# A pre-norm attention and GEGLU block: VectorE's additions of a split exp given to accumulating DMAs, more tiles for VectorE, and a second chunk cut in two

## The chip, the cores and the metric

The kernel runs on one core of a Trainium2 chip. A core has a matrix engine (TensorE, PE in the profile), VectorE (DVE), ScalarE (ACT), GpSimd (POOL) and SyncE (SP, which here only starts DMAs), each with its own queue of instructions that it works through in order; semaphores order the engines among each other. The metric is the device time of one execution in microseconds, the median of several runs.

## The reference

For 2048 rows of 640 numbers in bf16 (batch 1, 32 heads of 20):

```
x  = A_x
n  = layernorm(x)                       # no gain, no bias
q, k, v = split(n @ wqkv)               # 32 heads of 20
p  = softmax(q k^T / sqrt(20))          # 2048 x 2048 per head
h  = x + concat(p v) @ wo
m  = layernorm(h)
h2 = h + (gelu_tanh(m @ w_gate) * (m @ w_up)) @ w_down   # inner width 1728
```

The scores are 32 x 2048 x 2048 = 134 million numbers, and each goes through an exp.

## The kernel before

**Units of work.** Queries are worked on in chunks (`SIZES`: 512, 512, 256, 256, 256, 128, 128 rows). Four heads make a group, whose four small products lie side by side in TensorE. A tile is one PSUM bank of scores of one head: 128 keys on the partitions, 512 columns, which are 512 queries of one key block, or 256 queries of two key blocks, or 128 of four. A quad is the tiles of one group and key block for its four heads. A slot is one group of a chunk of 512, two groups of a chunk of 256, four of a chunk of 128: always 16 quads or 64 tiles, and there are 32 slots, 2048 tiles. No maximum is taken from the scores: a bound per query is put into one row of the operands beforehand.

**Two engines make the exp.** Most tiles go to ScalarE, two or three banks in one instruction (`unit`, the `exp` activation). Slots in `SIX` (8 to 15) use six banks for scores, in two halves of three; where a tile for VectorE is due there, it takes the third bank of the unit, and ScalarE's instruction takes two. In the other slots the halves have three and two banks, and VectorE's tile goes to bank 7 or 5, which the background work shares. `D_QUADS` says how many quads of each slot go to VectorE (68 in all, 272 tiles), `D_LEAD` how many tiles ahead of their slot these begin: 24 for most slots from slot 11 on.

**VectorE's exp** (`d_exp`) works in integer arithmetic on the bits of the number. L881 takes a tile out of PSUM, scaled, as int16 `v`. When two tiles (slots below `D_WIDE` = 18, "narrow", 128x1024) or four (from slot 18 on, "wide", 128x2048) are there, six instructions follow: `df` is the fraction of `v`'s bits; `dw` a linear function of it; `dw` squared; `dw` times `df`; `v` plus `dw`; and a scaling of `v` by 0.25 with an offset (called the rescaling below), after which the bits are those of a bf16 number. All six are on VectorE. The results are kept in a few buffers (`dv0`, `dv`, `dvw`) until the product with V takes them, at least `D_LAG` units later.

**The background.** While exps run, TensorE also does the products of probabilities and V (`pv_op`, accumulated in bank 6), and behind each chunk `post`: the output projection, the layer norm (its root in a run of small instructions on POOL, `ln_rsqrt`), transposes by DMA on SP's queue, and the MLP: gate products, a copy by VectorE, one gelu for the chunk on ScalarE (which has to load another function table for it, and the exp's again behind it), up products, VectorE's multiplication, `down`, the store. At the end of the last chunk the same is done without other work beside it (`tail`).

**The order.** The program records all operations with their reads, writes, banks, priorities and assumed durations, and `Sched.schedule` plays them through once, taking on each engine the ready operation of the best priority. What comes out is a fixed order for each queue, with semaphore waits (`emit`). So a changed number in the tables at the top moves instructions on all engines. Where TensorE would be idle for long, the planner puts in fillers: products with zeros (`sc.pad`) or thrown away ones (`sc.warm`).

The lines that matter in the profile: L366 is the helper through which most instructions of VectorE, ScalarE and POOL are recorded; L947 the score products; L881 the evacuation of VectorE's tiles; L1039 the transposes of the attention output; L1048 its division; L663 the projections; L1120 the gate and up products; L1155 and L1169 their copies and multiplications by VectorE; L1200 and L1204 the down products and the last addition.

Of the kernel before, what the change touches and what calls it, by code (L numbers as in the profile page):

```python
# [307 lines left out]
D = 640  # L308
# [6 lines left out]
NG = H // 4  # L315
SIZES = (512, 512, 256, 256, 256, 128, 128)
BASE = (0, 0, 0, 2, 0, 2, 3)
SIX = tuple(range(8, 16))
CHUNKS = tuple((sum(SIZES[:i]), n) for i, n in enumerate(SIZES))
# [10 lines left out]
PV_QUADS = 2  # L330
D_LAG = 9
MERGE = ()
PR, PR2 = 12, 6
D_QUADS = (1,) + (2,) * 15 + (2, 2) + (3, 2) * 5 + (2, 2, 2, 2)
D_FIRST, D_PART = 2, 0.75
D_LEAD = ((0,) * 8, (0, 10, 20) + (24,) * 21)
D_WIDE = 18
# [7 lines left out]
def bass_sequential_preLN__mha_block__glu_gated_geglu__prompt_kernel(  # L345
# [12 lines left out]
    with ExitStack() as es:  # L358
# [3 lines left out]
        def sb(name, shape, dt=BF16):  # L362
            return es.enter_context(nc.sbuf_tensor(name, shape, dt))
# [16 lines left out]
        identf = sb("identf", [128, 128], FP32)  # L380
        sel = sb("sel", [128, NA, H])
        zer = sb("zer", [128, 32])
        sel0 = sb("sel0", [128, 4, 32])
        off0 = sb("off0", [128, 1], FP32)
# [15 lines left out]
        pts = sb("pts", [128, PR * 512])  # L400
        osb = sb("osb", [128, 2, 512], FP32)
        rc = sb("rc", [128, 2, 16], FP32)
        o_nat = sb("o_nat", [128, 4, D])
        sq = sb("sq", [128, 512])
        xn_t = sb("xn_t", [128, 2, D])
        dvx = sb("dvx", [128, 1024])

# [21 lines left out]
        qoff = carve(512)  # L429
        aq = [carve(512) for _ in range(2)] + [sq[:], xn_t[:, 0, 0:512], xn_t[:, 1, 0:512]]  # L430
        carve = carver(regw, W_WORDS)
# [24 lines left out]
        df1 = carve(1024)  # L456
        dw1 = carve(1024).bitcast(F16)
        carve = carver(qt_all[:, 0, :, :].rearrange("p g s -> p (g s)"), NG * 512)
        dvw += [carve(2048).bitcast(I16) for _ in range(2)]
        dv.append(dvx[:].bitcast(I16))  # L460
        zb = dvx[:].rearrange("p (i s) -> p i s", i=2)
        dv0 = [ha_f[:, 1024 * i:1024 * i + 1024].bitcast(I16) for i in range(5)]
        df0, dw0 = ha_f[:, 5120:6144], ha_f[:, 6144:7168].bitcast(F16)
        carve = carver(qt_all[:, 1, :, :].rearrange("p g s -> p (g s)"), NG * 512)
        df2 = carve(2048)
        dw2 = carve(2048).bitcast(F16)
        carve = carver(qt_all[:, 2, :, :].rearrange("p g s -> p (g s)"), NG * 512)
# [9 lines left out]
        def bank(b, n=512):  # L477
            return PS[:, 512 * b.b:512 * b.b + n]
# [7 lines left out]
        def cst(fn, key, n=128):  # L486
            op(POOL, fn, 0.1 + n * 0.001, P_BG, writes=[key, "pool"])
# [19 lines left out]
        for g in range(1, NG, 2):  # L507
            cst(I("memset", f32(qt_all[:, 0, g:min(g + 2, NG), :]), 0.0), "qf0%d" % g, 512)
        cst(I("memset", sel[:], -1.0), "sel", 160)
        cst(I("affine_select", out=sel[:], in_=sel[:], compare_op=ALU.is_ge, fill=0.0, base=0,  # L510
              pattern=[[128, NA], [-DH, H]], channel_multiplier=1), "sel", 160)
        cst(I("affine_select", out=sel[:], in_=sel[:], compare_op=ALU.is_ge, fill=0.0, base=DH - 1,
              pattern=[[-128, NA], [DH, H]], channel_multiplier=-1), "sel", 160)
        cst(I("memset", sel0[:], 0.0), "sel0")
        cst(I("memset", off0[:], 0.0), "off0", 1)
# [76 lines left out]
        def ln_apply(eng, src, dst, dkey, t, rkeys, prio, first=False):  # L592
            if eng == "act":
                fn = I("activation", dst, src, ACT.Identity, bias=nm[:, t:t + 1], scale=rs[:, t:t + 1])
            else:
                fn = I("tensor_scalar", dst, src, mu[:, t:t + 1], rs[:, t:t + 1], ALU.add if first else ALU.subtract,
                       ALU.mult)
            return op(eng, fn, 0.82 if eng == "act" else c_dve(D, 0.46), prio,
                      reads=list(rkeys) + [("mu", t), ("rs", t)] + ([("nm", t)] if eng == "act" else []), writes=[dkey])

# [67 lines left out]
        def aqk(t):  # L668
            return ("xn", t - 3) if t >= 3 else ("aq", t)

# [98 lines left out]
        def q_bound0(banks, prio):  # L769
            bk = Bank(*banks)  # L770
            key = ("bk", sc_id())
            w_readers.append(op("pe", lambda eng: eng.matmul(
                bank(bk), sel0[:].rearrange("p j e -> p (j e)"), aq[0], start=True, stop=True),
                c_mm(512), prio, mode="full", util=0.213, reads=[("aq", 0), "sel0"], writes=[key], acq=[bk]))
            dst = qt_all[:, 0, 0, :]
            q_first.append(op("dve", lambda eng: eng.scalar_tensor_tensor(
                out=dst, in0=bank(bk), scalar=off0[:, 0:1], in1=dst, op0=ALU.add, op1=ALU.add), c_dve(512) + 0.05, prio,
                reads=[key, "off0"] + q_keys[0][0], writes=[("qo", 0, 0)], rel=[bk]))
            q_keys[0][0] = [("qo", 0, 0)]
# [70 lines left out]
        d_last = {}  # L850
        d_cur = [None]
        d_late = []
        d_pv = {}
# [8 lines left out]
        def d_exp(b, tile, prio, u):  # L862
# [5 lines left out]
            if h == 0:  # L868
                busy = set(x[1][1] for x in d_done)
                pool = [(kind, i) for i in range(5 if kind != "w" or CHUNKS[slots[units[u][0][0]][0]][0] >= 1536 else 3)]  # L870
                pool = [p for p in pool if p not in busy]
                assert pool
                d_cur[0] = min(pool, key=lambda p: d_last.get(p, -1))
                d_last[d_cur[0]] = len(d_ops)
            i = d_cur[0]
            v = {"e": dv0, "l": dv, "w": dvw}[kind][i[1]]
            df, dw = {"e": (df0, dw0), "l": (df1, dw1), "w": (df2, dw2)}[kind]
            keys = [("dv", i)] + ([("dv", ("l", k)) for k in ((0, 1), (2, 3), ())[i[1]]] if kind == "w" and i[1] < 3 else [])
            aft = tuple(e_ops) + (q_done(0) if c else ()) + (q_done(1) + tuple(d_late) if kind == "w" else ()) + \
                (q_done(2) if kind == "w" and i[1] > 2 else ())  # L880
            d_ops.append(op("dve", lambda eng: eng.tensor_scalar(v[:, 512 * h:512 * h + 512], bank(b), EXP_MUL, -32000.0,  # L881
# [5 lines left out]
            if h < n - 1:  # L887
                return
            zi = df.bitcast(I16)
            w_ = len(d_raw) / 2  # L890
            d = lambda fn, n, r, w: d_ops.append(op("dve", fn, 0.066 + n * w_, prio, reads=r, writes=w))
            d(I("tensor_scalar", zi, v, 511, 2048, ALU.bitwise_and, ALU.bitwise_or), 0.265, [("dv", i)], ["df"])
            d(I("tensor_scalar", dw, zi, CA / OCT, CB, ALU.mult, ALU.add), 0.265, ["df"], ["dw"])
            d(I("tensor_tensor", dw, dw, dw, ALU.mult), 0.53, ["dw"], ["dw"])
            d(I("tensor_tensor", dw, dw, zi, ALU.mult), 0.53, ["df", "dw"], ["dw"])
            d(I("tensor_tensor", v, v, dw, ALU.add), 0.53, ["dw", ("dv", i)], [("dv", i)])
            d(I("tensor_scalar", v, v, 0.25, 16256.0 + 128.0 * (CC - 1.0), ALU.mult, ALU.add), 0.265, [("dv", i)], [("dv", i)])
# [126 lines left out]
        def epilogue(s_, bk, d_sums):  # L1024
# [3 lines left out]
            nt = nq // 128  # L1028
            op("dve", I("tensor_copy", osb[:, s, :], PS[:, 512 * 6:512 * 7]), c_dve(512), P_QK,
               reads=[("O", s_)], writes=[("osb", s)], rel=[bk], after=tuple(d_sums))  # L1030
            b2 = Bank(*BGC[c])
# [6 lines left out]
            for tt in range(4):  # L1038
                op("pe", lambda eng, tt=tt: eng.transpose(bank(b2)[:, tt * 128:(tt + 1) * 128],  # L1039
                                                          osb[:, s, tt * 128:(tt + 1) * 128], identf[:]),  # L1040
                   c_mm(128, 2.5), P_EPI, mode="full", reads=[("osb", s), "identf"], writes=[key], acq=[b2] if tt == 0 else [],
                   after=tuple(aft) if tt == 0 else ())
# [22 lines left out]
        def post(c, first_banks, banks, tail):  # L1065
# [33 lines left out]
            for tt in range(tb, tb + nt):  # L1099
                t = q0 // 128 + tt - tb  # L1100
                ln_apply("dve", h_sb[:, tt, :], xn_t[:, t % 2, :], ("xn", t % 2), t, [("h", tt, 0), ("h", tt, 1)], pd)
                if tail:
                    transposes(xn_t[:, t % 2, :], [("xn", t % 2)], hnT[:, :, tt * 128:(tt + 1) * 128], ("hnT", tt),
                               first_banks, p, "act", after=first)
                else:
                    dma_transposes(xn_t[:, t % 2, :], [("xn", t % 2)], hnT[:, :, tt * 128:(tt + 1) * 128], ("hnT", tt),
                                   after=first)
# [188 lines left out]
```

## Time and profile before

| | us |
|---|---|
| median of 3 runs (914.05 to 917.4) | 914.34 |
| profiled execution, own time | 916.19 |
| profiled execution, span | 914.2 |
| ScalarE busy | 881.1 (96%) |
| TensorE busy | 824.1 (90%) |
| VectorE busy | 794.1 (87%) |
| GpSimd busy | 48.2 (5%) |

The span is the time from the first to the last instruction of the profiled execution; its own time has what lies around the span as well. The first exp starts at 33.3 us, the last one ends at 881.6 us. Instructions of one engine overlap a little at their ends, so a mean duration is longer than the distance from one start to the next; a "pace" below is that distance. The granted TensorE clock was 0.998 of full speed.

In a line of a group, the columns are: source line, engine, operation, output and input tensor with shape and type, count, busy time, mean duration in ns, and the idle time of the engine just before these instructions with what ended it. In a timeline: start, duration, engine, line, operation. In a line of DMA issues: count, size of one, median us from issue to landing.

### The profile page before, as it was taken

To read this page: it belongs to the slowest core of one execution; us is meant where nothing else is said; L and a number is where in the kernel's file an instruction comes from. 1 tells how busy PE (TensorE), PEld (TensorE's weight loads), DVE (VectorE), ACT (ScalarE), POOL (GpSimd) and SP (SyncE) were. 2 spreads that over 40 slices of the span, in tenths; PEclk is the share of its full clock that TensorE was granted. 3 is DMA by queue.
4 is the path that set the end of the run, shared out by engine and by line. 5 is a ranking of instruction groups with operands and counts; after the bars stand their busy time and mean duration, and the time that the engine had idled before them with its cause. 6 is when DMAs were issued, how large, how long until landed. Compare 5 with 4: busy or idle time off the path is not lost.

```text
span 914.2 us, 22759 instructions
## 1 busy us (share of the span) xinstructions
PE 824.1 (90%) x9952; PEld 351.2 (38%) x10017; DVE 794.1 (87%) x1458; ACT 881.1 (96%) x789; POOL 48.2 (5%) x149
## 2 busy tenths in 40 slices
PE   3999999999898878899798989999999989998998
PEld 1432322222232222233233333344454445556666
DVE  8869998999899986987899997999998998779753
ACT  7999999999999999999999999999999999999982
POOL 5000000000011000000021000002010000010000
PEclk9999999999999999999999999999999999999999
DMA  7211020323801000000122000000100000110000
GB/s 259 83 31 33 23 62 25 90 67 76 291 25 30 1 1 1 1 8 16 37 35 27 1 1 1 16 30 10 37 16 18 29 1 3 36 27 10 10 17 15
DMA packets 39514, 34.33 MB, mean 38 GB/s; under 512 B 19436, under 2 KB 36936, under 8 KB 39416
## 3 DMA queue, kind: packets, MB, share of 16 engines
q1 hardware_dynamic: 39416, 32.89, 12.9%
q8 instruction: 78, 1.28, 0.6%
q14 instruction: 20, 0.16, 0.1%
HBM read 20.12 MB, written 8.09 MB: 31 GB/s over the span
## 4 chain that ended last, share of the span: by engine, by line
ACT 57%; PE 23%; DVE 17%; POOL 1%; issue 1%; DMA 0%; DVEq 0%
ACT pts L366 36%; ACT rege L366 19%; PE ps L947 6%; DVE qt_all L366 5%; PE ps L366 4%; PE ps L1120 4%; PE ps L663 4%; PE ps L1200 3%; DVE rege L366 3%; DVE qt_all L881 2%; DVE rege L881 2%; DVE rege L1169 1%; DVE rege L1155 1%; ACT L366 1%; DVE regw L701 1%
## 5 line engine op out<-in xcount | busy, mean ns | idle before, releaser
L366 ACT ACTIVATE pts<-ps 128x1024 bf16<-128x1024 f32 (+1 forms) x470 | 561.6, 1349 | 3.6 <-PE ps L947 1.5
L947 PE MATMUL ps<-qt_all,kt_all 32*128 32x256 bf16 (+2 forms) x3584 | 309.2, 289 | 44.8 <-ACT pts L366 22.0
L366 ACT ACTIVATE rege<-ps 128x1024 bf16<-128x1024 f32 (+1 forms) x233 | 288.9, 1342 | 1.9 <-PE ps L366 1.3
L947 PEld LDWEIGHTS ps<-qt_all,kt_all 32*128 32x128 bf16 x3584 | 101.4, 92 | 265.1 <-ACT pts L366 135.6
L366 DVE TENSOR_TENSOR qt_all<-qt_all 128x2048 f16<-128x2048 f16 (+3 forms) x186 | 175.0, 941 | 2.6
L1120 PE MATMUL ps<-rege,regw 128*128 128x256 bf16 (+2 forms) x952 | 151.0, 288 | 12.1 <-ACT rege L366 3.5
L366 PE MATMUL ps<-pts,v_all 128*21 128x256 bf16 (+2 forms) x2070 | 125.4, 291 | 0.4 <-DVE osb L366 0.4
L881 DVE TENSOR_SCALAR qt_all<-ps 128x512 int16<-128x512 f32 x128 | 87.4, 683 | 20.0 <-PE ps L947 19.5
L1120 PEld LDWEIGHTS ps<-rege,regw 128*128 128x128 bf16 x980 | 72.5, 98 | 71.2 <-issue 30.5
L881 DVE TENSOR_SCALAR rege<-ps 128x512 int16<-128x512 f32 x128 | 87.5, 684 | 11.0 <-PE ps L947 10.3
L366 PE MATMUL ps<-rege,v_all 128*21 128x256 bf16 (+2 forms) x1214 | 91.9, 294 | 2.6 <-DVE rege L366 2.3
L663 PE MATMUL ps<-regw 128*128 128x320 bf16 (+1 forms) x340 | 82.5, 353 | 4.2 <-ACT regw L611 1.7
L366 DVE TENSOR_SCALAR qt_all<-qt_all 128x1024 f16<-128x1024 int16 (+2 forms) x153 | 84.0, 557 | 1.9
L1200 PE MATMUL ps<-regw,rege 128*128 128x320 bf16 x448 | 80.6, 302 | 2.0 <-DVE rege L1169 1.0
L366 DVE TENSOR_TENSOR rege<-rege 128x1024 f16<-128x1024 f16 (+1 forms) x90 | 61.4, 683 | 0.8
L366 PEld LDWEIGHTS ps<-pts,v_all 128*21 128x21 bf16 x2070 | 45.1, 91 | 34.8 <-issue 29.3
L1169 DVE TENSOR_TENSOR rege<-rege,ps 128x512 bf16<-128x512 bf16 (+1 forms) x53 | 35.6, 677 | 21.9 <-PE ps L1120 21.8
L1200 PEld LDWEIGHTS ps<-regw,rege 128*128 128x128 bf16 x448 | 36.3, 97 | 34.4 <-issue 16.0
L366 DVE TENSOR_SCALAR rege<-rege 128x1024 int16<-128x1024 int16 (+2 forms) x115 | 48.3, 436 | 0.5
L366 PE MATMUL ps<-kt_all,zer 128*32 128x512 bf16 x560 | 46.9, 384 | 0.0
L663 PEld LDWEIGHTS ps<-regw 128*128 128x128 bf16 x360 | 28.4, 99 | 45.0 <-issue 24.5
L366 PEld LDWEIGHTS ps<-rege,v_all 128*21 128x21 bf16 x1214 | 31.1, 91 | 22.6 <-issue 12.1
(105 smaller groups left out, 587.9 us busy)
## 6 DMA issues: line engine op xcount, KB each, us to landing
rege<-in_A_x_dram SPq DMA_DIRECT2D x6, 640.0 KB, 5.2
q_rows<-regw SPq DMA_DIRECT2D x20, 128.0 KB, 1.7
out_dram<-rege SPq DMA_DIRECT2D x16, 160.0 KB, 2.5
regw<-in_B_w_gate_dram SPq DMA_DIRECT2D x1, 2160.0 KB, 8.4
regw<-in_B_w_up_dram SPq DMA_DIRECT2D x1, 2160.0 KB, 13.4
regw<-in_B_w_down_dram SPq DMA_DIRECT2D x1, 2080.0 KB, 19.8
kt_all<-k_rows SPq DMA_DIRECT2D x12, 160.0 KB
qt_all<-q_rows SPq DMA_DIRECT2D x12, 160.0 KB
```

The costliest lines, as they stand in the source:

```text
L366: return lambda eng: getattr(eng, method)(*args, **kwargs)
L663: yield op("pe", lambda eng, l=l, r=r, k=k: eng.matmul(bank(bk, n), l, r, start=(k == 0), stop=(k == len(steps) - 1)), c_mm(n) + cold, pri ...
L701: e = op("dve", lambda eng: eng.tensor_copy(dst, bank(bk)), c_dve(512), prio, reads=[key], writes=[dkey], rel=[bk], after=after)
L881: d_ops.append(op("dve", lambda eng: eng.tensor_scalar(v[:, 512 * h:512 * h + 512], bank(b), EXP_MUL, -32000.0, ALU.mult, ALU.max), c_dve( ...
L947: return lambda eng: eng.matmul(out()[:, kk * nq:(kk + 1) * nq], kt_all[32 * j:32 * j + 32, g, kt * 128:(kt + 1) * 128], qt_all[32 * j:32 ...
L1120: op("pe", lambda eng, a=a, f=f, fi=fi: eng.matmul(bank(bk)[:, fi * nq:(fi + 1) * nq], w[:, a, F0[f]:F0[f] + 128], hnT[:, a, 128 * tb:128 ...
L1155: cp.append(op("dve", lambda eng, bg=bg, fv=fv, w=w: eng.tensor_copy(fv, bank(bg, w)), c_dve(w), p, reads=[kg], writes=hkeys(k), rel=[bg], ...
L1169: hdone.append(op("dve", lambda eng, bu=bu, fv=fv, w=w: eng.tensor_tensor(fv, fv, bank(bu, w), ALU.mult), c_dve(w), p, reads=[ku] + hkeys( ...
L1200: op("pe", lambda eng, f=f, o=o, hf=hf, bk=bk: eng.matmul(bank(bk, 320), ha_f[:, o:o + 128], wd[:, f, hf * 320:(hf + 1) * 320], start=(f = ...
```

## The change

- VectorE's fifth instruction (`v` plus `dw`) is dropped for tiles of the slots in `DA_SLOTS` (all but 0, 4, 6, 7 and 8). The fourth instruction writes its product as int16, and a DMA started from POOL's queue adds it to `v` (`accum_op`). The rescaling on VectorE then waits for that DMA. There are two buffers for `dw` in turns, where there was one. The planner is given 0.95 us for the issue and up to 6.2 us for the landing.
- 75 quads instead of 68 go to VectorE: three in most slots from 18 on.
- VectorE's tiles of slot 11 and later begin 54 tiles ahead of their slot, instead of 24.
- Chunk 1 (512 rows) becomes two chunks of 256 rows; there are 8 chunks. Six banks for scores only in slots 8 to 11.
- Buffers: `sq`, `xn_t` and one half of `osb` go; their space makes one more narrow buffer for results (six instead of five), one or more wide ones (four or six instead of three or five), and the second `dw`. The normalized rows of the second layer norm now go into `o_nat`, the |q| rows and `sel` into the new `dvx` and `dwx`.
- `D_LAG` is 8 instead of 9, `D_PART` 0.65 instead of 0.75.

```diff
-SIZES = (512, 512, 256, 256, 256, 128, 128)
-BASE = (0, 0, 0, 2, 0, 2, 3)
-SIX = tuple(range(8, 16))
+SIZES = (512, 256, 256, 256, 256, 256, 128, 128)
+BASE = (0, 0, 2, 0, 2, 0, 2, 3)
+SIX = tuple(range(8, 12))
...
-D_LAG = 9
+D_LAG = 8
 MERGE = ()
+DA_ISSUE, DA_LAT = 0.95, 6.2
+DA_SLOTS = (1, 2, 3, 5) + tuple(range(9, 32))
 PR, PR2 = 12, 6
-D_QUADS = (1,) + (2,) * 15 + (2, 2) + (3, 2) * 5 + (2, 2, 2, 2)
-D_FIRST, D_PART = 2, 0.75
-D_LEAD = ((0,) * 8, (0, 10, 20) + (24,) * 21)
+D_QUADS = (1,) + (2,) * 15 + (2, 2) + (3,) * 10 + (3, 2, 3, 2)
+D_FIRST, D_PART = 2, 0.65
+D_LEAD = ((0,) * 8, (0, 10, 20) + (54,) * 21)
...
-        osb = sb("osb", [128, 2, 512], FP32)
+        osb = sb("osb", [128, 512], FP32)
...
-        sq = sb("sq", [128, 512])
-        xn_t = sb("xn_t", [128, 2, D])
-        dvx = sb("dvx", [128, 1024])
+        dvx = sb("dvx", [128, 2048])
+        dwx = sb("dwx", [128, 2048])
...
-        dw1 = carve(1024).bitcast(F16)
+        dw1 = [carve(1024), dwx[:, 1024:2048]]
...
-        dw2 = carve(2048).bitcast(F16)
+        dw2 = [carve(2048), dwx[:]]
...
+            d_alt[0] += 1
+            a_ = d_alt[0] % len(dw)
+            dk = ("dw", a_)
+            dw = dw[a_]
+            di, dw = dw.bitcast(I16), dw.bitcast(F16)
...
-            d(I("tensor_tensor", dw, dw, zi, ALU.mult), 0.53, ["df", "dw"], ["dw"])
-            d(I("tensor_tensor", v, v, dw, ALU.add), 0.53, ["dw", ("dv", i)], [("dv", i)])
+            if tile[0] in DA_SLOTS:
+                d(I("tensor_tensor", di, dw, zi, ALU.mult), 0.53, ["df", dk], [dk])
+                d_ops.append(op(POOL, I("dma_start", v, di, accum_op=ALU.add), DA_ISSUE, prio, reads=[dk], writes=[("dv", i)],
+                                sem="da%s%d" % i, lat=DA_LAT * (w_ + 1) / 3))
+            else:
+                d(I("tensor_tensor", dw, dw, zi, ALU.mult), 0.53, ["df", dk], [dk])
+                d(I("tensor_tensor", v, v, dw, ALU.add), 0.53, [dk, ("dv", i)], [("dv", i)])
             d(I("tensor_scalar", v, v, 0.25, 16256.0 + 128.0 * (CC - 1.0), ALU.mult, ALU.add), 0.265, [("dv", i)], [("dv", i)])
...
-                ln_apply("dve", h_sb[:, tt, :], xn_t[:, t % 2, :], ("xn", t % 2), t, [("h", tt, 0), ("h", tt, 1)], pd)
+                ln_apply("dve", h_sb[:, tt, :], o_nat[:, tt, :], [("on", g, tt) for g in range(NG)], t, [("h", tt, 0), ("h", tt, 1)], pd)
```

## The prediction, made before the changed kernel ran

> **What bounds the kernel now.** I read the page's shares first: ScalarE is busy 96% of the span, TensorE 90%, VectorE 87%. A mean over stages hides which one binds where, so the second view is the table of stretches: before the first exp (0 to 33.3 us), four pieces of the exp stream, and the tail behind the last exp (881.6 us).
>
> ```profile
> span 914.2 us, 22759 instructions
> 33.30:266.00 232.70, 216.09 (x1774) 67.39 (x1793) 209.28 (x422) 230.43 (x203) 0.62 (x1) 1.00 0.26 77
> 266.00:450.00 184.00, 158.54 (x1332) 49.12 (x1353) 158.48 (x308) 183.94 (x155) 8.04 (x28) 1.00 0.05 12
> 450.00:660.00 210.00, 193.47 (x2562) 80.94 (x2575) 197.09 (x324) 209.24 (x183) 14.54 (x42) 1.00 0.09 17
> 881.60:914.20 32.60, 27.99 (x381) 22.98 (x379) 13.18 (x32) 11.02 (x14) 0.00 (x0) 1.00 0.05 16
> 33.30:881.60 848.30, 777.47 (x9439) 317.38 (x9501) 752.95 (x1345) 842.64 (x727) 35.28 (x113) 1.00 0.12 32
> ```
>
> Columns: stretch, length, then busy time (and instructions) of PE, PE weight loads, DVE, ACT, POOL, then clock, DMA share, GB/s. From 33.3 to 881.6 us ScalarE works 842.6 of 848.3 us: it is the bound there, 5.7 us idle in all. VectorE is idle 95 us in the same stretch. In the last 32.6 us ScalarE works only 11 and TensorE 28.0: the tail is TensorE's.
>
> The third view, the groups by shape, prices ScalarE's work; the fourth, the chain of waits, gives the pace of instructions that overlap by their fill.
>
> ```profile
> L366 ACT ACTIVATE pts<-ps 128x1536 bf16<-128x1536 f32 x249 | 377.3, 1550 | 3.4 <-PE ps L947 1.5 <-PE ps L366 0.9
> L366 ACT ACTIVATE pts<-ps 128x1024 bf16<-128x1024 f32 x221 | 243.9, 1122 | 0.2
> L366 ACT ACTIVATE rege<-ps 128x1536 bf16<-128x1536 f32 x121 | 185.4, 1551 | 1.9 <-PE ps L366 1.3 <-PE ps L947 0.4
> L366 ACT ACTIVATE rege<-ps 128x1024 bf16<-128x1024 f32 x112 | 124.2, 1116 | 0.0
> L366 ACT ACT_TABLE_LOAD x16 | 20.5, 1283 | 1.0 <-PEq L1281 0.8
> 695.49 4.52 ACT pts L366 x4
> 700.01 2.26 ACT rege L366 x2
> ```
>
> A pair (one exp of three tiles, one of two) takes 2.26 us; the means differ by 0.43 us, so three tiles pace at 1.34 us and two at 0.92.
>
> **Step 1, fewer tiles on ScalarE: -12.4 us.** VectorE takes 75 quads of 4 tiles instead of 68, so ScalarE's 2048 - 272 = 1776 tiles become 1748. With six banks now in slots 8 to 11 only, the grouping changes too: in the compiled order ScalarE's exps go from 370 of three tiles and 333 of two (703) to 353, 344 and a single one (698). 17 x 1.34 - 11 x 0.92 - 0.5 = 12.2; these paces add up to 802 us where the trace has about 808 (842.6 less 12.8 of loads and 21.6 of gelus), so I scale to 12.4. It lies on the bound, with nothing beside it.
>
> **Step 2, the second chunk as two of 256: +2.6 us on ScalarE.** One more chunk means one more trip to the gelu table and back inside the stream: 12 loads there instead of 10, 2 x 1.28 us. Gelu elements and instructions (14) stay. TensorE gets twice the matmuls of half the width in that chunk: five of 512 columns take 1.25 us, (1.25 - 0.38)/4 = 0.22 each; twenty of 256 take 2.36, or 0.11 each. So a split matmul costs nothing; its weight loads double, and the stretch 450 to 660, already all chunks of 256, shows ScalarE at 209.2 of 210. I price the rest of the split at 0 (cover: TensorE's fillers, 560 matmuls on zeros; were it gone, the 0.7 us by which that stretch's idle time exceeds that of the one before). SP's queue issues one load of x less, and the same stores and transposes.
>
> **Step 3, VectorE's additions go: -23 us on VectorE, 0 on the end by itself.** The timeline at two places gives an addition's pace, the start of the next less its own:
>
> ```profile
> 507.35 1.21 DVE L366 TENSOR_TENSOR rege<-rege,qt_all 128x2048 int16<-128x2048 int16 x1
> 508.48 0.68 DVE L881 TENSOR_SCALAR qt_all<-ps 128x512 int16<-128x512 f32 x1
> 267.04 0.68 DVE L366 TENSOR_TENSOR qt_all<-qt_all 128x1024 int16<-128x1024 int16 x1
> 267.63 0.48 DVE L1087 TENSOR_TENSOR rege<-ps,rege 128x320 bf16<-128x320 f32 x1
> ```
>
> 1.13 us wide, 0.60 narrow. In the compiled order 40 wide and 52 narrow additions become DMAs (18 narrow stay): 45 + 31 = 76 us. Seven more wide quads cost 4 x 0.60 + 3 x 0.61 + 3 x 1.13 = 7.6 us each, 53 us. Net -23.
>
> **Step 4, a wait in VectorE's queue instead: up to 22 us of it, 0 on the end.** The rescaling of a quad now waits for its DMA, and VectorE runs in order: behind it stand the evacuations of score banks (L881) and of the MLP, TensorE waits for those banks, ScalarE for TensorE. What covers it is other VectorE work: counting the compiled order at the trace's paces, between the multiplication that makes the addend and the rescaling lie 7.7 us in the median for wide ones (least 2.4) and 4.3 for narrow (least 1.5). The trace has no accumulating DMA and none issued by POOL. Nearest rows, issue to landing:
>
> ```profile
> rege<-in_A_x_dram SPq DMA_DIRECT2D x6, 640.0 KB, 5.2
> rege<-in_A_x_dram SPq DMA_DIRECT2D x3, 320.0 KB, 3.1
> regw<-in_B_w_gate_dram SPq DMA_DIRECT2D x1, 2160.0 KB, 8.4
> out_dram<-rege SPq DMA_DIRECT2D x16, 160.0 KB, 2.5
> ```
>
> A narrow addend is 256 KB, a wide one 512 KB; both also read the destination. Lower ends: 2.5 us narrow, 3.1 wide (the rows below their sizes): waits of 3 us in all. Upper ends: 5.9 and 9.1 (the rows from twice the size up, plus 0.7 for a delayed issue, below): 87 + 72 = 159 us. I take the rows nearest in size, 3.1 and 5.2, plus 0.7: 3.8 and 5.9. Then 17 narrow ones wait 14.9 us and 5 wide ones 7.5, 22 us, about what Step 3 freed; so ScalarE's 5.7 us of idle time stay.
>
> The 0.7 us is a blocked POOL instruction, beside a VectorE addition that began at 267.04:
>
> ```profile
> 267.07 0.69 POOL L366 CAST mu<-mv 128x2 f32<-128x2 bf16 x1
> 267.70 0.18 POOL L366 CAST nw<-sd 128x2 f32<-128x2 bf16 x1
> ```
>
> The cast ends when the addition does. VectorE pays nothing in that run (its rescaling at 268.04 takes 0.41 us like its group), though the Trainium skill, SBUF — State Buffer, § Who interferes with whom, lets either one block the other, whichever is first. The same page speaks against this change: a DMA issued from GpSimd has its descriptors written there, and they starve while VectorE runs an instruction that takes both ports; by its example (620 ns alone, 3100 beside a copy) each landing would be some 2.5 us later and the sum slower. That POOL is held up, the trace agrees; that a DMA is, no run here shows.
>
> POOL's queue takes 92 issues among the layer norm's chains (14 instructions, 4.7 us at 266.6); POOL is 95% idle, and those chains feed the MLP, which has slack until the tail. Cost 0; without that slack, a chain's length once per chunk. The 33 MiB the DMAs add go to engines that are 5 to 10% busy from 266 us on.
>
> **Step 5, 54 tiles of lead, six banks in four slots, buffers: 0.** VectorE's tiles of a slot are made one slot earlier, so in the last slot VectorE has none; total work is unchanged. Cover: five or six buffers for the results, where four or five stood; if they run out, an evacuation (0.60 us) waits.
>
> **Step 6, the tail: +5.6 us.** Here the order decides. Before, behind the last scores matmul (880.0 us) TensorE has 260 MLP matmuls of 128 columns and 68 of 320. After, chunk 5's gelu comes 6 exps before the end (before, the last such gelu came 32 before), and TensorE has 39 of 256 columns, 220 of 128 and 112 of 320 left.
>
> ```profile
> 879.96 1.80 PE L1200 MATMUL ps<-regw,rege 128*128 128x320 bf16 x12
> 895.82 2.06 PE L1200 MATMUL ps<-regw,rege 128*128 128x320 bf16 x14
> 898.96 7.99 PE L1120 MATMUL ps<-rege,regw 128*128 128x128 bf16 x140
> 907.46 3.98 PE L1200 MATMUL ps<-regw,rege 128*128 128x320 bf16 x28 [0.51 <-DVE rege L1145]
> ```
>
> Paces: 7.99/140 = 0.056 us; 3.98/28 = 0.14; 0.11 from Step 2. Before: 14.6 + 9.5 + 3.4 (last PV, transposes, output projection) = 27.5 of 31.4 us, 4 us idle or filled. After: 4.3 + 12.3 + 15.5 + 3.4 = 35.5, and with that much to do the norm's chain (15 us before, from PV's end to the MLP) is covered; I leave 1.5 us for the two waits on VectorE's products. 37.0 - 31.4 = +5.6. Bounds: +4 (no idle time) to +8 (the 4 us stay).
>
> **Sum.** -12.4 + 2.6 + 5.6 = -4.2 us: a span of 910.0 for 914.2. The profiled execution took 916.19 with that span, 1.85 above the median of 914.34; against the median the forecast is 910.1, say 910.
>
> **The rivals.**
> - *The tail gives nothing back* and the early waits go: exps end 9.8 us sooner, the MLP keeps up, ScalarE's 1.2 us idle at 75 to 100 us disappear. 914.3 - 11 = 903 to 907. For it: TensorE's 560 fillers. Against: the order, which is fixed.
> - *Late sums* (slower): DMAs land 0.7 us later than I took, 4.5 and 6.6 us. VectorE then waits 31 + 12 = 43 us, 20 more than Step 3 freed, and where it is already full (24.9 of 25 us at 625 to 650) that stops score banks and so ScalarE: 910 + 18 = 928. It decides from about 4.1 and 6.2 us on; at the upper ends, 159 - 23 - 95 = 41 us even after all VectorE's idle time, 951. For it: two reads per element, the blocked cast. Against: distances of 7.7 us for wide ones. The lock in the Trainium skill, SBUF — State Buffer, § Who interferes with whom, would lead here.
> - *Small waits*: half of that, 915 to 919, no change.
>
> **How the numbers follow.** My case has 0.55 (906 to 914), the first rival 0.17, small waits 0.06, late sums 0.22. 0.5% is 4.6 us, about what a measurement can tell from no change; 909.8 cuts my own case in half. Faster 0.28 + 0.17 = 0.45; same 0.27 + 0.06 = 0.33; slower 0.22. The range reaches into both ends: 904 to 922.
>
> **What would show it.** Right: ScalarE with 698 exps, about 790 us of paces, the last exp near 872 us; a tail near 38 us with TensorE busy throughout; waits of VectorE on DMA below 25 us in all; POOL issues landing near 4 and 6 us. Wrong: ScalarE idle far above 6 us with waits on score matmuls held by VectorE, a landing beyond 6.6 us wide, or a tail as short as before.

## The result, and the profile after

The changed kernel takes 922.52 us in the median (ten runs, 917.82 to 924.07), the kernel before 915.64 beside it (ten runs, 914.05 to 917.40). The ratio is 1.0074, with a 95% interval of 1.0063 to 1.0084: slower by 0.7%, where 910 was forecast. The profiled execution took 923.45 us with a span of 921.3 and a mean granted clock of 0.987 (before: 0.998).

The page of the changed kernel, its first part and the two large DMA queues (packets, MB, share of 16 engines' time):

```profile
span 921.3 us, 25281 instructions
PE 834.2 (91%) x11185; PEld 387.4 (42%) x11232; DVE 773.4 (84%) x1444; ACT 868.9 (94%) x784; POOL 130.4 (14%) x241
...
q0 software_dynamic: 13248, 34.61, 20.8%
q1 hardware_dynamic: 39432, 32.89, 13.2%
```

ScalarE's busy time fell from 881.1 to 868.9 us and VectorE's from 794.1 to 773.4, yet the span grew by 7.1. The work did go away; something else came in. The table of stretches of the changed kernel (length, then busy time of PE, PE weight loads, DVE, ACT, POOL, then clock, DMA share, GB/s) says in which part:

```profile
33.16:883.62 850.46, 781.61 (x10636) 348.74 (x10681) 729.07 (x1327) 833.02 (x724) 117.37 (x205) 0.99 0.35 73
883.62:921.30 37.68, 34.12 (x416) 27.85 (x414) 16.20 (x37) 8.35 (x13) 0.00 (x0) 1.00 0.05 19
275.00:300.00 25.00, 19.58 (x277) 7.35 (x279) 20.92 (x46) 23.19 (x21) 8.42 (x19) 0.93 0.46 73
450.00:475.00 25.00, 23.03 (x323) 10.95 (x322) 17.51 (x38) 23.76 (x22) 3.86 (x8) 1.00 0.54 96
825.00:850.00 25.00, 23.11 (x447) 12.88 (x444) 13.55 (x25) 19.04 (x17) 4.32 (x16) 0.73 0.41 64
```

The tail is as forecast. In the stretch of the exps ScalarE works 833.0 of 850.5 us: 17.4 us idle, where the kernel before had 5.7. The loss is not even: 6.0 us of it lie between 825 and 850 us, 1.8 between 275 and 300, 1.2 between 450 and 475 (a fourth place, 2.3 us from 625 to 650, has another cause and is taken up near the end). In the first two the mean clock is 0.73 and 0.93. In the kernel before, the stretch from 825 to 850 us was whole:

```profile
825.00:850.00 25.00, 22.37 (x488) 15.00 (x487) 22.04 (x37) 24.94 (x22) 2.59 (x14) 1.00 0.08 14
```

In the changed kernel ScalarE waits for scores from TensorE (L965), and TensorE for transposes (engine, tile and line, what it waits for: us in total, times, longest):

```profile
ACT pts L368 <- PE ps L965: 8.0, 10, 1.3
ACT rege L368 <- PE ps L965: 4.0, 5, 1.6
PE ps L1138 <- DMA rege<-o_nat: 2.8, 2, 1.4
PE ps L667 <- DMA rege<-o_nat: 2.2, 2, 1.7
```

Before, the first two were 1.5 and 0.4 us, and TensorE waited once, 0.6 us, for a transposition. VectorE is not what holds TensorE up there: its waits for the accumulating DMAs come to 2.1 us in the whole run.

```profile
DVE qt_all L368 <- DMA qt_all<-qt_all: 1.4, 2, 1.2
DVE dvx L368 <- DMA dvx<-qt_all: 0.7, 2, 0.5
```

The worst place, 822 to 848 us, as a timeline of the changed kernel (start, duration, engine, line, operation, and in brackets the idle time before it with its releaser):

```profile
826.66 0.87 POOL L368 DMA_DIRECT2D dvx<-qt_all  x1 [5.76 <-DVE qt_all L368]
...
828.50 1.90 SPq L368 DMA_TRANSPOSE rege<-o_nat  x1
...
834.31 0.69 PE L667 MATMUL ps<-wo,rege 128*128 128x320 bf16 x2 [1.71 <-DMA rege<-o_nat]
...
835.58 1.02 ACT L368 ACTIVATE rege<-ps 128x1024 bf16<-128x1024 f32 x1 [1.63 <-PE ps L965]
...
837.74 1.45 ACT L368 ACTIVATE pts<-ps 128x1536 bf16<-128x1536 f32 x1 [1.14 <-PE ps L965]
```

POOL starts an addition of 512 KB at 826.66. SP starts the transposition of the attention output behind it, at 828.50. The output projection (L667) needs that transposition, and TensorE, which works in order, stands idle for 1.71 us in front of it, with score products queued behind. The DMA issues of these ten microseconds (826 to 836; count, size, us from issue to landing):

```profile
dvx<-qt_all POOLq DMA_DIRECT2D x1, 512.0 KB, 6.8
out_dram<-rege SPq DMA_DIRECT2D x1, 160.0 KB, 2.4
rege<-o_nat SPq DMA_TRANSPOSE x1, 5.7
```

The kernel before has a median of 2.7 us for both of its groups of transposes:

```profile
rege<-xn_t SPq DMA_TRANSPOSE x15, 2.7
rege<-o_nat SPq DMA_TRANSPOSE x11, 2.7
```

Here this one takes 5.7 us. The same microseconds of the changed kernel in stretches of three:

```profile
828.00:831.00 3.00, 3.00 (x91) 1.83 (x89) 1.17 (x5) 3.00 (x4) 0.00 (x0) 1.00 1.00 182
831.00:834.00 3.00, 1.42 (x26) 0.64 (x23) 2.72 (x5) 2.95 (x3) 0.00 (x0) 1.00 1.05 53
834.00:837.00 3.00, 2.69 (x44) 1.37 (x44) 1.05 (x2) 1.02 (x1) 0.00 (x0) 0.50 0.02 5
837.00:840.00 3.00, 3.00 (x43) 1.58 (x43) 1.62 (x2) 2.00 (x2) 0.00 (x0) 0.50 0.00 0
840.00:843.00 3.00, 3.00 (x60) 1.89 (x61) 2.27 (x3) 1.76 (x2) 0.00 (x0) 0.50 0.00 0
```

Two things are to be seen. From 828 to 834 us all DMA engines are taken (share 1.00 and 1.05), though the mean share of the exp stretch is 0.35; SP's queue, with the transposition, takes 53% of their time in these six microseconds, POOL's queue, with the addition, 48.5%. And behind the wait the clock is 0.50 from 834 to about 847.6 us: TensorE is busy nearly all the time and does 43 to 60 matmuls in 3 us where it did 91 (of mixed sizes), and ScalarE is fed too slowly. Of the 6.0 us that ScalarE loses here, 1.6 come directly behind TensorE's wait; nearly all of the rest comes in five pieces while the clock is low.

The mean clock gives a size for the second effect over the run, as an estimate: with 0.987 over 921.3 us, (1 - 0.987) x 921.3 / 0.5 = 24 us were run at half clock; before, 0.998 makes 3.7 us. The ten runs of the changed kernel go with it: those at 0.994 and 0.993 have spans of 916.1 and 917.1 us, those at 0.987 to 0.985 have 920.6 to 922.3.

### The profile page after: what moved, and what is told of

Same layout as the page of the kernel before. It is cut to its first block, busy times and chain, and to the rows that moved or that the text cites. A ratio compares the mean times of both kernels' runs of the same rounds, so it can differ in the third digit from the quotient of the medians.

```text
span 921.3 us, 25281 instructions
## 1 busy us (share of the span) xinstructions
PE 834.2 (91%) x11185; PEld 387.4 (42%) x11232; DVE 773.4 (84%) x1444; ACT 868.9 (94%) x784; POOL 130.4 (14%) x241
## 4 chain that ended last, share of the span: by engine, by line
ACT 52%; PE 28%; DVE 11%; DMA 4%; POOL 2%; issue 1%; SPq 0%; DVEq 0%
ACT pts L368 34%; ACT rege L368 18%; PE ps L965 8%; PE ps L1138 6%; PE ps L368 5%; PE ps L667 5%; PE ps L1218 3%; DMA rege<-o_nat 2%; DVE qt_all L368 2%; DVE dwx L368 2%; DVE qt_all L889 2%; DMA regw<-in_A_wqkv_dram 1%; DVE rege L889 1%; POOL nw L368 1%; DVE dvx L889 1%
## 5 line engine op out<-in xcount | busy, mean ns | idle before, releaser
L368 ACT ACTIVATE pts<-ps 128x1536 bf16<-128x1536 f32 (+1 forms) x466 | 552.5, 1336 | 10.7 <-PE ps L965 8.0
L965 PE MATMUL ps<-qt_all,kt_all 32*128 32x256 bf16 (+2 forms) x4096 | 315.6, 275 | 40.7 <-ACT pts L368 20.8
L368 ACT ACTIVATE rege<-ps 128x1536 bf16<-128x1536 f32 (+1 forms) x232 | 287.0, 1342 | 6.5 <-PE ps L965 4.0
L965 PEld LDWEIGHTS ps<-qt_all,kt_all 32*128 32x128 bf16 x4096 | 109.0, 93 | 247.7 <-ACT pts L368 122.2
L1138 PEld LDWEIGHTS ps<-rege,regw 128*128 128x128 bf16 x1120 | 86.0, 98 | 67.8 <-issue 28.6
L889 DVE TENSOR_SCALAR qt_all<-ps 128x512 int16<-128x512 f32 x124 | 85.0, 686 | 16.8 <-PE ps L965 15.8
L889 DVE TENSOR_SCALAR rege<-ps 128x512 int16<-128x512 f32 x120 | 82.1, 686 | 18.6 <-PE ps L965 17.7
L667 PE MATMUL ps<-regw 128*128 128x512 bf16 (+1 forms) x343 | 82.5, 352 | 4.0 <-DMA regw<-in_A_wqkv_dram 1.3
L368 DVE TENSOR_TENSOR qt_all<-qt_all 128x2048 int16<-128x2048 f16 (+3 forms) x81 | 76.6, 945 | 0.8
L368 DVE TENSOR_SCALAR qt_all<-qt_all 128x2048 int16<-128x2048 int16 (+3 forms) x116 | 66.7, 577 | 2.6 <-DMA qt_all<-qt_all 1.4
L368 PEld LDWEIGHTS ps<-pts,v_all 128*21 128x21 bf16 x2318 | 52.9, 92 | 32.2 <-issue 27.7
L368 PE MATMUL ps<-kt_all,zer 128*32 128x512 bf16 x640 | 55.6, 390 | 0.0
L368 DVE TENSOR_TENSOR rege<-rege 128x1024 f16<-128x1024 f16 (+1 forms) x74 | 50.6, 684 | 0.8
L1218 PEld LDWEIGHTS ps<-regw,rege 128*128 128x128 bf16 x448 | 37.7, 98 | 31.8 <-issue 14.1
L368 POOL DMA_DIRECT2D qt_all<-dwx x26 | 25.0, 960 | 182.9 <-DVE dwx L368 166.3
L667 PEld LDWEIGHTS ps<-regw 128*128 128x128 bf16 x360 | 28.9, 99 | 44.8 <-issue 23.4
```

Source lines behind the costliest of these rows:

```text
L368: return lambda eng: getattr(eng, method)(*args, **kwargs)
L667: yield op("pe", lambda eng, l=l, r=r, k=k: eng.matmul(bank(bk, n), l, r, start=(k == 0), stop=(k == len(steps) - 1)), c_mm(n) + cold, pri ...
L965: return lambda eng: eng.matmul(out()[:, kk * nq:(kk + 1) * nq], kt_all[32 * j:32 * j + 32, g, kt * 128:(kt + 1) * 128], qt_all[32 * j:32 ...
L1138: op("pe", lambda eng, a=a, f=f, fi=fi: eng.matmul(bank(bk)[:, fi * nq:(fi + 1) * nq], w[:, a, F0[f]:F0[f] + 128], hnT[:, a, 128 * tb:128 ...
L1218: op("pe", lambda eng, f=f, o=o, hf=hf, bk=bk: eng.matmul(bank(bk, 320), ha_f[:, o:o + 128], wd[:, f, hf * 320:(hf + 1) * 320], start=(f = ...
```

## The experiments

The theory that these traces suggest is called Q, for queueing: the bytes of the additions delay the transposes on the DMA engines, TensorE waits in order, its clock falls, ScalarE starves. Its rival is O, for order: 75 quads, the split chunk, six banks in fewer slots or 54 tiles of lead leave VectorE or TensorE short, wherever the bytes go. Within Q there is a second question: whether each byte costs, wherever it lies. The quoted text of each experiment was written before its run. Each ratio is to runs of the kernel before that were measured beside it (medians 914.70 to 915.71 us).

### Additions of 32 columns, same order

```diff
-I("dma_start", v, di, accum_op=ALU.add)
+I("dma_start", v[:, 0:32], di[:, 0:32], accum_op=ALU.add)
```

> The changed kernel with every instruction in the same order, but each accumulating DMA moves only the first 32 of its 1024 or 2048 columns; the rest of the sum is left out. Theory Q (queueing: the additions fill the DMA engines, the DMA transposes behind the layer norm land late, TensorE waits for them in order, its granted clock falls to 0.5, ScalarE idles): transposes land at 2.7 us again, clock at least 0.996, ScalarE's idle time in the exp stream falls from 16 to about 6 us, time 910 to 914 us. Theory O (order: 75 quads, the split chunk and the longer lead leave TensorE or VectorE short wherever the bytes go): same clock 0.987, 920 us or more.

Measured: 912.86 us (ten runs), ratio to before 0.9978 (0.9966 to 0.9990). Stretches of this kernel:

```profile
33.16:872.99 839.83, 774.67 (x10636) 346.25 (x10681) 727.64 (x1327) 831.61 (x724) 117.15 (x205) 1.00 0.15 33
872.99:910.70 37.71, 34.11 (x416) 27.84 (x414) 16.18 (x37) 8.34 (x12) 0.00 (x0) 1.00 0.05 19
275.00:300.00 25.00, 20.31 (x306) 7.79 (x313) 22.85 (x50) 25.00 (x23) 8.41 (x19) 1.00 0.19 30
825.00:850.00 25.00, 24.45 (x605) 15.34 (x603) 19.29 (x35) 25.00 (x23) 4.33 (x16) 1.00 0.17 30
```

Instructions, order and issues are those of the changed kernel; only bytes are gone. 9.7 us go with them (922.52 - 912.86). The places at 275 and 825 us are whole again, at full clock, and the transposes land in 2.7 us as before (the one that took 5.7 us takes 3.3); TensorE waits 0.3 us for one in all. Q holds for these 9.7 us, and O can explain no more than what is left: ScalarE is still idle 8.2 us here.

### Transposes expected later

The planner is told that a transposition lands after 4.6 us instead of 2.0, so it puts the projection later.

```diff
-op("sp", I("dma_start_transpose", dst, src), ..., lat=2.0, after=after)
+op("sp", I("dma_start_transpose", dst, src), ..., lat=4.6, after=after)
```

> The changed kernel, the planner told that a DMA transpose lands 4.6 us after its issue instead of 2.0, so that TensorE's products behind it are put later in its order; the DMAs are untouched. Theory Q: the late landings no longer hold up TensorE, clock at least 0.995, 909 to 915 us. Theory O: nothing in it changes the load, 920 us or more.

Measured: 922.54 us (four runs), ratio 1.0086 (1.0054 to 1.0118): missed. The last exp ends at 873.3 us, 10 us earlier, and TensorE has no wait for a transposition in this trace, though they land after 3.3 us in the median. But the planner moved the MLP of one more chunk, with its gelu, behind the last exp:

```profile
873.30:924.90 51.60, 47.22 (x563) 39.62 (x561) 23.39 (x49) 14.32 (x17) 0.00 (x0) 1.00 0.06 17
```

The tail of this kernel is 51.6 us instead of 37.7: what the stream gained, the tail gave back. A planner's number changes the whole order, so this run proves nothing on Q by its time. The clock falls here too (0.76 from 700 to 725 us), without any wait for a transposition: such waits are not the only thing that it falls behind.

### All additions on VectorE

```diff
-DA_SLOTS = (1, 2, 3, 5) + tuple(range(9, 32))
+DA_SLOTS = ()
```

> The changed kernel with all additions on VectorE as before, 75 quads, lead of 54 and split chunk kept. Theory Q: no additions in the DMA engines, transposes at 2.7 us and clock at least 0.994, but VectorE has 76 us more to do, some 815 us of paces in an exp stream of 840, and now stops ScalarE: 915 to 922 us. Theory O: as the changed kernel or worse, 922 us and more, clock 0.987 or lower.

Measured: 939.02 us (four runs), ratio 1.0261 (1.0244 to 1.0278), where Q expected 915 to 922: slower, but by far more. A wait of ScalarE and the tail of this kernel:

```profile
ACT rege L368 <- DVE rege L1173: 23.5, 3, 15.8
881.70:938.00 56.30, 52.44 (x594) 42.75 (x593) 26.79 (x57) 14.15 (x16) 2.56 (x14) 1.00 0.09 28
```

VectorE is busy 844.2 us here. The exps do not end later than in the changed kernel (881.7 us); what is longer is the tail, 56.3 us for 37.7. Gelus wait for VectorE's copies, and two of these three waits, 21.6 us, lie behind the last exp, where one more chunk's MLP is left, as in the run before. The transposes land after 2.7 us. So with 75 quads the additions are better off VectorE, even at what they cost as DMAs; but the order is another one, and the run does not separate the theories by its time.

### Only the additions, in the structure of before

Chunks, six banks, quads, lead, `D_PART` and `D_LAG` as before; additions by DMA as changed.

```diff
-SIZES = (512, 256, 256, 256, 256, 256, 128, 128)
-BASE = (0, 0, 2, 0, 2, 0, 2, 3)
-SIX = tuple(range(8, 12))
+SIZES = (512, 512, 256, 256, 256, 128, 128)
+BASE = (0, 0, 0, 2, 0, 2, 3)
+SIX = tuple(range(8, 16))
...
-D_LAG = 8
+D_LAG = 9
...
-D_QUADS = (1,) + (2,) * 15 + (2, 2) + (3,) * 10 + (3, 2, 3, 2)
-D_FIRST, D_PART = 2, 0.65
-D_LEAD = ((0,) * 8, (0, 10, 20) + (54,) * 21)
+D_QUADS = (1,) + (2,) * 15 + (2, 2) + (3, 2) * 5 + (2, 2, 2, 2)
+D_FIRST, D_PART = 2, 0.75
+D_LEAD = ((0,) * 8, (0, 10, 20) + (24,) * 21)
```

> Only the additions by DMA (and the buffers they need): chunks, six banks, 68 quads, lead, lag as before. Nothing is taken from ScalarE. Theory Q: some transposes land late, clock 0.99 to 0.997, 914 to 919 us. Theory O: the additions are harmless and VectorE is relieved of 76 us, 912 to 914.5 us, clock 0.998.

Measured: 933.04 us (four runs), ratio 1.0204 (1.0172 to 1.0235): both theories missed. The clock of the profiled run, the fastest of the four, is 0.998, so there it is not the falling clock. ScalarE waits in this kernel for another line:

```profile
ACT pts L368 <- PE ps L368: 13.0, 5, 5.8
ACT rege L368 <- PE ps L368: 9.9, 4, 4.8
```

These are the products with V, which free the buffers of ScalarE's probabilities. Before the longest of these waits, 5.8 us, TensorE's order has a product with a tile of VectorE, at 712.06 us, ahead of those with ScalarE's, at 714.17. The next run varies this.

### The same with 54 tiles of lead

```diff
-D_LEAD = ((0,) * 8, (0, 10, 20) + (24,) * 21)
+D_LEAD = ((0,) * 8, (0, 10, 20) + (54,) * 21)
```

(against the kernel of the experiment before)

> As e5 (chunks, six banks, 68 quads as before, additions by DMA), but VectorE's tiles begin 54 ahead as in the changed kernel. If the 24 tiles of lead were too few for results that come a DMA later, e5's 17 us go: 914 to 919 us, ScalarE's waits for the products with V below 6 us where e5 has 23. If not (the additions themselves cost it), 928 us and more.

Measured: 926.03 us (four runs), ratio 1.0119 (1.0100 to 1.0137). 7.0 us came back, and the two waits above fell from 22.9 to 4.5 us; so that part of the reading holds. Expected were 914 to 919. What is left goes with Q's signs, though no run with short additions was made in this structure: the clock is 0.992, TensorE waits 4.8 us for transposes, and ScalarE is idle 2.5 to 3.4 us in each of the stretches of 25 us from 450, 650 and 825 us. With 68 quads, additions by DMA, the buffers they need and the longer lead cost 11.3 us against the kernel before, measured beside it (914.70).

### 68 quads in the changed kernel

```diff
-D_QUADS = (1,) + (2,) * 15 + (2, 2) + (3,) * 10 + (3, 2, 3, 2)
+D_QUADS = (1,) + (2,) * 15 + (2, 2) + (3, 2) * 5 + (2, 2, 2, 2)
```

> The changed kernel with 68 quads as before. ScalarE gets 28 tiles back, +12.4 us in its stream; behind the last scores TensorE has 23.8 us of work left instead of 35.5, -11 us. With the same falls of the clock as the changed kernel: 922 us; with fewer, since VectorE has 53 us less to do: 913 to 917 us.

Measured: 933.71 us (four runs, 928.23 to 938.66), ratio 1.0223 (1.0181 to 1.0266): missed, and it speaks against the part of O by which 75 quads are too many for VectorE. In the profiled run, the fastest of the four, the last exp ends at 895.9 us, 12.3 later than with 75 quads. ScalarE works 845.3 us in the stream, 12.3 more, which is Step 1's 12.4, and is idle as long as there (17.4 us); the tail is 7.4 us shorter. Why the other three runs take 3 to 10 us more is not known; their clock is lower (0.984 to 0.993 for 0.996).

### Short additions in the last four slots alone

```diff
-I("dma_start", v, di, accum_op=ALU.add)
+I("dma_start", v if tile[0] < 28 else v[:, 0:32], di if tile[0] < 28 else di[:, 0:32], accum_op=ALU.add)
```

> The changed kernel with every instruction in the same order; only the additions of slots 28 to 31 move 32 columns instead of 2048 (the rest of those sums is left out), all others are whole. Theory Q, localized: the transposes near 828 us land in time, the fall of the clock at 834 to 847 us goes, those near 280 and 450 us stay: ScalarE 6 us less idle, 916 to 918 us, clock 0.993 to 0.995. Theory O: no change, 922 us.

Measured: 915.98 us (ten runs), ratio 1.0013 (1.0000 to 1.0027), as expected. Stretches of this kernel:

```profile
275.00:300.00 25.00, 20.21 (x282) 7.31 (x279) 20.71 (x46) 22.95 (x21) 8.40 (x19) 0.93 0.44 70
825.00:850.00 25.00, 24.65 (x588) 15.29 (x585) 18.95 (x36) 25.00 (x23) 4.29 (x16) 1.00 0.21 36
```

The place at 825 us is whole, the one at 275 as bad as before the edit. 6.5 of the 9.7 us (5.6, when each kernel is taken against the runs of before beside it) come from the additions of slots 28 to 31, which are 10 of the 92: a cost with a place, not one per byte.

### Late slots relieved

Two quads fewer (73) in the last four slots, whose additions go back to VectorE.

```diff
-DA_SLOTS = (1, 2, 3, 5) + tuple(range(9, 32))
+DA_SLOTS = (1, 2, 3, 5) + tuple(range(9, 28))
...
-D_QUADS = (1,) + (2,) * 15 + (2, 2) + (3,) * 10 + (3, 2, 3, 2)
+D_QUADS = (1,) + (2,) * 15 + (2, 2) + (3,) * 10 + (2, 2, 2, 2)
```

> The changed kernel with two quads in each of slots 28 to 31 and their additions on VectorE, which has time there. Two quads back to ScalarE: +3.6 us; 29.3 instead of 35.5 us of TensorE's work left behind the last scores: -6; no addition near the last transposes, no fall of the clock at 834 us: -6. Theory Q: 912 to 917 us. Theory O: 919 us and more.

Measured: 918.16 us (six runs), ratio 1.0032 (1.0015 to 1.0048), 1 us above what was expected. The loss at 825 us is gone (24.3 of 25 busy, clock 1.00); the one at 275 us grew to 3.5 us (clock 0.80):

```profile
275.00:300.00 25.00, 20.70 (x262) 7.02 (x256) 19.67 (x42) 21.52 (x19) 8.38 (x19) 0.80 0.45 72
```

The wait there is that of the changed kernel, 1.3 us for 1.4, but the clock stays at half for some 10 us behind it instead of some 3.5.

### Half of each addition

```diff
-I("dma_start", v, di, accum_op=ALU.add)
+I("dma_start", v[:, 0:512 * len(d_raw) // 2], di[:, 0:512 * len(d_raw) // 2], accum_op=ALU.add)
```

> The changed kernel, same order, each addition moves half of its columns (the other half of the sums is left out). Theory Q with a queue whose length is what counts: transposes near 2.8 us, most of the 9.7 us between short and whole additions gone already, 913 to 917 us. If every byte cost the same, half: 917.5 us.

Measured: 913.39 us (ten runs), ratio 0.9985 (0.9972 to 0.9997). Half of the bytes take 9.1 of the 9.7 us away. In this kernel the wide additions land in 3.3 to 3.6 us, the transposes are where they were before the change, and TensorE waits 1.0 us for them in all:

```profile
qt_all<-dwx POOLq DMA_DIRECT2D x20, 256.0 KB, 3.6
...
rege<-o_nat SPq DMA_TRANSPOSE x26, 2.7
```

### Short transposes, whole additions

```diff
-I("dma_start_transpose", dst, src)
+I("dma_start_transpose", dst[:, 0:1, :], src[:, 0:128])
```

> The changed kernel with every instruction in the same order and all additions whole; each DMA transpose moves only the first 128 of its 640 columns (the rest of the layer norm's output and of the attention output is left out of what follows). Theory Q: what the additions cost goes through the transposes, so short ones land soon enough and the falls of the clock at 290 and 834 us go: 911 to 915 us, clock at least 0.995. If the additions cost their time in another way (VectorE's or POOL's waits, stores, loads of x): 919 us or more.

Measured: 914.28 us (ten runs), ratio 0.9995 (0.9983 to 1.0006), as Q expected. Stretches of this kernel:

```profile
275.00:300.00 25.00, 20.81 (x312) 8.14 (x313) 23.13 (x51) 24.84 (x22) 9.73 (x27) 1.00 0.29 49
825.00:850.00 25.00, 23.38 (x573) 14.47 (x575) 17.92 (x34) 24.18 (x22) 4.32 (x16) 1.00 0.34 74
```

The additions are whole and land as in the changed kernel (4.9 and 3.5 us); with transposes of a fifth, landing in 2.5 us, TensorE waits 0.6 us for them, and 8.2 of the 9.7 us are gone. So the additions cost little by themselves: nearly all of the cost goes through the transposes. It is not that late sums held up VectorE or its buffers, since the sums come as late as before.

### Late slots relieved, and chunk 0's normalized rows transposed on TensorE

The relieved kernel above, and the transposes of chunk 0's normalized rows as TensorE products that VectorE copies out (its attention output was transposed that way already), so four transposes by DMA less.

```diff
+PE_T = (0,)
...
-                if tail or c == 0:
+                if tail or c == 0 or c in PE_T:
...
-                if tail:
+                if tail or c in PE_T:
...
-                               first_banks, p, "act", after=first)
+                               first_banks, p, "act" if tail else "dve", after=first)
```

> The kernel of e16 (two quads in slots 28 to 31, their additions on VectorE), with the transposes of the first chunk's normalized rows on TensorE instead of by DMA, so that the fall of the clock near 280 us, 3.5 us of ScalarE's idle time in e16, has no transposes to come from. Theory Q: 912 to 916 us, clock 0.996. If that fall was made otherwise: 918 us as e16.

Measured: 913.14 us (ten runs, 912.28 to 915.12), ratio to before 0.9981 (0.9970 to 0.9991). Stretches of this kernel:

```profile
33.16:875.80 842.64, 794.90 (x10798) 352.14 (x10794) 728.78 (x1324) 835.32 (x728) 108.00 (x195) 1.00 0.32 67
875.80:911.20 35.40, 31.10 (x406) 25.21 (x403) 13.83 (x34) 11.03 (x14) 0.00 (x0) 1.00 0.06 20
275.00:300.00 25.00, 23.01 (x339) 8.46 (x340) 23.93 (x53) 25.00 (x23) 8.36 (x19) 1.00 0.31 54
825.00:850.00 25.00, 22.91 (x481) 14.17 (x478) 17.59 (x31) 24.94 (x23) 2.58 (x14) 1.00 0.14 16
```

Both places are whole, the clock is 0.998, ScalarE's idle time in the stretch is 7.3 us. It is a little faster than both kernels: 0.2% against before, some 1% against the change (913.14 to 922.52).

## Why the prediction was wrong

**Held.** Step 1: 353 exps of three tiles, 344 of two and a single one, and ScalarE works 833.0 us in the stretch where 842.6 - 12.4 + 2.6 = 832.8 was forecast; the run with 68 quads shows the 12.4 by itself (12.3). Step 2 is in that sum; it was not run alone. Step 3: VectorE's busy time fell by 20.7 us, forecast 23. Step 6: the tail is 37.7 us, forecast near 38. It is filled with MLP products to the end (timeline of the changed kernel):

```profile
897.64 7.94 PE L1138 MATMUL ps<-rege,regw 128*128 128x128 bf16 x137
905.42 3.97 PE L1218 MATMUL ps<-regw,rege 128*128 128x320 bf16 x28
909.22 4.80 PE L1138 MATMUL ps<-rege,regw 128*128 128x128 bf16 x83
```

**Step 4's wait was far smaller than forecast.** Landings were taken as 3.8 us narrow and 5.9 wide. The page of the changed kernel, its DMA issues:

```profile
qt_all<-dwx POOLq DMA_DIRECT2D x20, 512.0 KB, 4.9
rege<-rege POOLq DMA_DIRECT2D x16, 256.0 KB, 3.5
...
rege<-o_nat SPq DMA_TRANSPOSE x26, 3.1
```

3.5 and 4.9 us, and VectorE's waits are 2.1 us, not 22. Why so few is more than the shorter landings explain, and was not followed. POOL's queue, at 0.88 to 0.96 us per issue, held nothing up that shows in ScalarE's waits. So the 0 for this wait came out, but not because Step 3 paid for 22 us of it.

**The step that failed** is the last sentence of Step 4: "The 33 MiB the DMAs add go to engines that are 5 to 10% busy from 266 us on", costed at nothing. The share was a mean over stretches of a hundred microseconds and more. In the microseconds around a transposition the 16 engines are full (1.00 to 1.05 at 828 to 834 us), the transposition lands after 5.7 us instead of 2.7, and TensorE's fixed order has a product in front of the scores that needs it. TensorE waits for transposes four times, 5.0 us in all, where it waited once, 0.6 us. The short additions put this term at 9.7 us, and short transposes take 8.2 us of it away with the additions whole. The prediction followed the new DMAs to VectorE, which waits for them, but not to SP's transposes, which go beside them. Step 4's "0 on the end" therefore holds for the wait in VectorE's queue alone.

A sentence of the Trainium skill would have pointed there: DMA: Bandwidth & Descriptors, § Issuing engines are not separate DMA queues, says that DMAs started by different engines run on the same 16 DMA engines and interleave. The trace agrees: beside additions from POOL's queue the median of SP's transposes goes from 2.7 to 3.1 us, and one takes 5.7.

**A second, smaller term.** The forecast had the last exp at 881.6 - 12.4 + 2.6 = 871.8 us and a tail of 38.2. 921.3 - 910.0 = 11.3 us were missed: 11.8 in the end of the exps (883.6), -0.5 in the tail. The bytes are some 9.7 of that. With short additions ScalarE is still idle 8.2 us in the stream, 2.5 more than in the kernel before; the new pieces lie mainly at 50 to 125, 175 to 200 and 625 to 650 us (4.6 us together, less some 2 that the kernel before loses from 775 to 825 us). The last is the largest, here in the changed kernel:

```profile
625.00:650.00 25.00, 23.66 (x299) 10.68 (x292) 21.84 (x34) 22.71 (x21) 1.89 (x2) 0.86 0.33 63
```

There TensorE waits twice near 642 us, 0.5 and 0.4 us, for VectorE to empty a bank of scores (L889), the clock is at half for some 7 us behind it, and ScalarE is idle 2.3 us. With short additions it is the same (0.5 and 0.4 us, clock 0.86, 2.2 us), so the landings do not make it. In the kernel before VectorE was full there and ScalarE idle 0.2 us. Step 5's zero was too kind by about these 2.5 us; which of its parts, no run tells apart.

**The rivals.** None names this mechanism. *Late sums* came out on the side that happened, but by a wait of VectorE for its DMAs that comes to 2.1 us instead of 43. The lock of GpSimd's DMAs by VectorE that was weighed with it does not show either: additions of 8 KB, in an order in which VectorE is as busy, land in 2.0 to 2.3 us in the median, and no issue takes POOL longer than 1.4 us. *Small waits* forecast 915 to 919 by the same wait, halved; neither the time nor the wait came. *The tail gives nothing back* is excluded by the 37.7 us. The upper end of the range, 922, was drawn from waits of VectorE; that it lies so near the measured 922.5 is luck.

**Shown and argued.** Shown by runs: that the bytes cost 9.7 us, not in proportion, more than half of it in the last four slots, and nearly all of it only together with the transposes. Read from rows and not varied by itself: that the fallen clock makes most of it. The traces do hold waits for a transposition of nearly one length with different clocks behind them:

| kernel, end of the wait | TensorE's wait, us | then at half clock, us | ScalarE idle in the 25 us around it, us |
|---|---|---|---|
| changed kernel, 459 us | 1.42 | 0 | 1.2 |
| changed kernel, 291 us | 1.36 | some 3.5 | 1.8 |
| late slots relieved, 290 us | 1.34 | some 10 | 3.5 |
| changed kernel, 834 us | 1.71 | some 13.6 | 6.0 |

So ScalarE's loss is about the wait where the clock holds, and grows with the time at half clock where it does not. Span goes with clock over the ten runs too. What decides whether the clock falls behind such a wait, and for how long, no run here shows.

## What to carry to other kernels

A transfer that is "hidden" has two customers: the one that waits for it, and every other transfer on the same engines at that time. So look for short transfers with an in-order engine right behind them, and read the DMA share in stretches as short as a landing (3 us here, 1.00 against a mean of 0.35). Where TensorE is nearly full, price a wait in its queue as a range: here it cost ScalarE from 0.9 to 3.5 times its length, and the clock behind it in the trace tells which.

## What was not expected of the hardware

- The clock fell after a short wait and stayed low long. From 831 to 834 us TensorE was busy 1.42 of 3 us, with one wait of 1.71; the clock was then 0.50 for some 13.6 us, in which TensorE was busy 2.7 to 3.0 of every 3 us. At 288 to 294 us a similar gap (1.12 of 3 busy) was followed by only one stretch of 3 us at 0.55 and one at 0.89, and a wait of 1.42 us before 459 us (1.90 of 3 busy) by no fall at all. The Trainium skill, TensorE: Matmul & The Clock Gate, § What's actually happening, gives about 3.4 us of idling for the fall and about 3.4 us of work for the return; this trace has the half clock that it names, but a fall after a shorter gap, and in one place a return after four times that.
- The landing of additions has medians of 2 us and more even for few bytes, and grows by 2.6 to 2.9 us up to 512 KB: 2.0 to 2.3 us for 8 KB, 3.5 for 256 KB, 4.9 for 512 KB, with 0.9 us of POOL for each issue.
- No slowing of VectorE by POOL's issues shows: its scalings of 128x2048 int16 numbers, the rescaling among them, take 685 ns in the mean in the changed kernel and 678 before.
